# FFN1 eight slots behind the attention, its end blocks side by side, x split one pair a slot; w_in converted thinly, then densely; ten pairs by rows with float32 value products

## The chip, the cores and the metric

The kernel runs on one core of a Trainium2 chip. The time is that of the device, in microseconds (us), from launch to end; the kernel before took 1503.16 us, the median of three runs (1502.47 to 1505.43). The core has five engines that run their own instruction streams and wait for each other by semaphores: TensorE (PE; its weight loads are listed as PEld), VectorE (DVE), ScalarE (ACT), GpSimd (POOL) and SyncE (SP), which here only issues the transfers (DMAs). TensorE writes to PSUM, eight banks here called bank0 to bank7; the other tiles lie in SBUF.

## The reference

Attention with RMS-normalised queries and keys, and behind it a feed-forward network with a squared ReLU:

```python
q_n, k_n = (rmsnorm(q, g_q), rmsnorm(k, g_k))     # q, k, v: 8 x 12 x 448 x 64, float32
scores = scale * np.matmul(q_n, k_n.transpose(0, 1, 3, 2))
scores = scores - np.max(scores, axis=-1, keepdims=True)
attn = np.exp(scores)
attn = attn / (np.sum(attn, axis=-1, keepdims=True) + 1e-09)
out = np.matmul(attn, v)
x = out, laid out as 3584 tokens x 768
h = x @ w_in                                      # 768 x 2048
r = np.maximum(h, 0.0)
g = s * (r * r) + b
return g @ w_out                                  # 2048 x 768
```

w_in and w_out come as 64-bit floating-point numbers; the kernel rebuilds float32 values from their two words, which is called a conversion below.

## The kernel before

**Precision.** TensorE's fast format (float32r) keeps fewer bits than float32. A product is therefore made of three: high part by high part, high by low, low by high. So every large operand has to be split into a high part (a cast, mostly on ScalarE) and a low part (value minus high part, on VectorE or GpSimd). The float32 product is the other way: one instruction, without a split, that TensorE runs as two passes.

**Slots.** The 96 heads are 48 pairs (NPAIR), six to a batch (NP) of eight (B). The whole attention is one list of slots, written out by hand with a fixed order of instructions on all five engines (manual_schedule, L612). A pair has eight slots (W), four chunks of keys for each of its two heads; slot s handles chunk s. In a slot PE makes the transposed scores of the chunk in two products (score_t, L398), the scores in the other direction of the chunk ten slots ahead (score, L362; AHEAD), whose maximum VectorE takes (maximum, L374), and the value products of the chunk two slots before (weigh, L449). ScalarE takes the exponential (exponent). All other work of a pair is put at fixed distances from its first slot by at(...) in the loop at L565: loading, normalising and splitting its queries and keys before, and taking the sums, their reciprocals (gather, invert, divide, by way of DRAM) and the result u after. A job started in one slot may go on in the next ones, one step a slot (the list begun, L630). Jobs in the list late (L550) come last in the slot on VectorE and GpSimd.

**Two ways for queries and keys.** Pairs of the first batch (p < NP) come by rows: load_rows, norm_rows (square on ScalarE, sums on VectorE, power and scaling on GpSimd), turn (eight transpositions on PE a head) and split_turned. The others come already transposed and twice (load_kq), with their inverse roots computed from a second load (load, norm), kept in DRAM and spread over the partitions (keep, spread), multiplied in scale and split in split_kq.

**Two ways for the value products.** For the pairs p < NV, 12 here, exponentials and values stay float32 (load_v, weigh: one product a chunk). For the others exponentials are split (split_e on ScalarE, split_e_lo on VectorE), values too (split_v), and a chunk has three products, the last chunk of a head, which packs high and low parts into the same rows, two.

**FFN1.** ffn_in (L174) makes one block of 128 of the 2048 hidden columns for one batch: 6 x 3 matmuls into one bank. The 16 blocks of a batch are a stream from which each slot takes six matmuls (FILL = 2, 2, 2): 48 slots use up 288. The stream of batch b - 1 begins START = 13 slots behind that batch's last slot (L654). What it reads, x split into two parts, is made by split_x (L510), two pairs at a time, in the three slots before and at that begin. rectify applies the ReLU on ScalarE and frees the bank, keep_r stores the result in DRAM.

**w_in.** Its 24 pieces of 128 x 512 are loaded (load_piece, L530) and converted in slots s to s + 4 for each s in PACE (L32): four operations on VectorE, two on ScalarE, one on GpSimd (load_double, L116). Two buffers each hold the raw words (w64) and the value being built (wa). Six entries of PACE lie before slot 6, then one every five slots up to slot 91.

**Behind the slots.** FFN1 of the last batch runs alone on PE, while w_out is converted, 32 pieces, two a step (L731; later_by, four steps, is how far the last part of a conversion stands behind the others, since it writes over w_in). ffn_out (L697) then makes FFN2 from tiles g = s r^2 + b, three tiles together at first, then one by one; its instructions are ordered by the framework, not by hand.

Of the kernel before, what the change touches and what calls it, by code (L numbers as in the profile page):

```python
# [11 lines left out]
I32 = mybir.dt.int32  # L12
# [8 lines left out]

LEAST = (1 + 1 / 8) * 2.0 ** (0x70 - 127)

START = 13

AHEAD = 10

# [1 line left out]

FILL = (2, 2, 2)  # L30

PACE = (-18, -14, -10, -6, -2, 2, *range(6, 92, 5))  # L32

GAP = 2

# [2 lines left out]
def attention_then_relu2_ffn(  # L38
# [38 lines left out]
    NP = NPAIR // B  # L77
    H = 2 * NP
    TILES = 2 * SEQ // P
    NV = 2 * NP  # L80
    NQ = 4
    QC = SEQ // NQ
    REST = SEQ % P
# [87 lines left out]
    xp = ctx.enter_context(tc.tile_pool(name="xpool", bufs=1))  # L171
    later = []

    def ffn_in(xs, b, fc):  # L174

        i, f0 = divmod(fc * P, FS)
        ph, bank = psum(f"ph{b}_{fc}")
        n = 0
        for cc in range(NCC):
            for w, part in ((whi[i], 0), (wlo[i], 0), (whi[i], 1)):  # L180
                T.matmul(  # L181
                    ph[:, :SEQ],
                    w[:, cc, f0 : f0 + P],
                    xs[b, cc][:, part, :],
                    start=n == 0,
                    stop=n == 3 * NCC - 1,
                )
                n += 1
                if n == 3 * NCC:
                    later.append((ph, bank, b, fc))  # L190
                yield

    def rectify():

# [15 lines left out]
    with tc.tile_pool(name="apool", bufs=1) as ap:  # L210
# [296 lines left out]

        xs = {}

        def split_x(b, k):  # L510
            for g in (2 * k, 2 * k + 1):
                u = us.pop(b * NP + g)
                x = xs[b, g] = xp.tile([P, 2, SEQ], F32R, tag=f"x{g}", name=f"x{b}_{g}")
                S.copy(x[:, 0, :], u)
                V.tensor_tensor(x[:, 1, :], u, x[:, 0, :].bitcast(F32), ALU.subtract)  # L515

        def pieces():
            for i, (hi, lo, src) in enumerate(parts_of_w_in()):
# [15 lines left out]
                next(g)  # L534
                loaded.append(g)

        def convert(n):


            g = loaded[0] if n == 0 else turning[0]  # L540
            if n == 0:
                turning.append(loaded.pop(0))
            for _ in range((2, 1, 1, 2, 1)[n]):
                next(g, None)
            if n == 4:
                turning.pop(0)

        turning = []

        late = (convert, invert)  # L550

# [12 lines left out]

        for p in range(NPAIR):  # L565
            s0 = W * p
            if p >= NP:
                at(s0 - 32, load, p)
                at(s0 - 28, norm, p)
                at(s0 - 24, keep, p)  # L570
            for j in range(2):
                s1 = s0 + 4 * j
                if p >= NP:
                    at(s1 - 19, load_kq, p, j)
                    at(s1 - 19, spread, p, j)
                    at(s1 - 15, scale, p, j)
                    at(s1 - 13, split_kq, p, j)
                else:
                    at(max(s1 - 28, FIRST), load_rows, p, j)
                    at(s1 - 20, norm_rows, p, j)  # L580
                    at(s1 - 13, turn, p, j)
                    at(s1 - 12, split_turned, p, j)
                at(s1 - 10, double_kb, p, j)
                at(s1 - 6, shift, p, j)
                at(s1 + 6, take, p, j)
                at(s1 + 7, gather, p, j)
            at(s0 - (9 if p >= NV else 5), load_v, p)
            if p >= NV:
                at(s0 - 3, split_v, p)
            at(s0 + 13, invert, p)  # L590
            at(s0 + 14, divide, p, 1)
            at(s0 + 16, divide, p, 2)
            at(s0 + 18, divide, p, 3)
        for b in range(B):
            for k_ in range(3):
                at(W * NP * (b + 1) + START - 2 + k_, split_x, b, k_)
        for _ in range(2):
            at(FIRST + 1, load_piece)
        for s_ in PACE:
            for n in range(5):  # L600
                at(s_ + n, convert, n)
            at(s_ + 3, load_piece)

        def within(i):
# [6 lines left out]
        sb_b = cpool.tile([P, 1], F32, name="sb_b")  # L611
        with tc.manual_schedule(engines=ORDERED):  # L612
            begun = []
            for s_ in range(FIRST, NSLOT + START + 1):
                if s_ == FIRST:
                    nc.sync.dma_start(gg, g_qk)
                    V.scalar_tensor_tensor(gqk, gg[:, 0:1], D**-0.5, gg[:, 1:2], ALU.mult, ALU.mult)
                if s_ == 0:
                    for t, x in ((sb_s, s), (sb_b, b_)):
                        nc.sync.dma_start(t, x.rearrange("(o d) -> o d", o=1).broadcast_to([P, 1]))  # L620
                if s_ in (FIRST, FIRST + 4):
                    warm_up(30)
                if within(s_):
                    score_t(s_)
                filler(FILL[0])
                if within(s_ - 1):
                    split_e(s_ - 1)
                if within(s_):
                    exponent(s_)
                begun = [g for g in begun if next(g, 0) is None]  # L630
                keep_r()
                for f, a in jobs[s_]:
                    if f in late:
                        continue
                    g = f(*a)
                    if g is not None and next(g, 0) is None:
                        begun.append(g)
                ahead = s_ + AHEAD
                scored = within(ahead)
                if scored:  # L640
                    score(ahead)
                filler(FILL[1])
                rectify()
                if within(s_ - 1):
                    split_e_lo(s_ - 1)
                if scored:
# [12 lines left out]
            rectify()
            keep_r()  # L660


    with tc.tile_pool(name="opool", bufs=2) as op:

        def pieces():
            for i, part in enumerate(parts_of_w_out()):
                w = op.tile([P, WO, 2], I32, tag="w64", bufs=4, name=f"w64o{i}")
                m = op.tile([P, WO], F32, tag="wm", bufs=2, name=f"wmo{i}")

                def words(i=i):  # L670
                    return op.tile([P, WO], I32, tag="wa", bufs=10, name=f"wao{i}")

                yield load_double((w, words, m), *part, apart=True, rest=V)

# [47 lines left out]
        pieces = pieces()  # L722


        later_by = NFC // NS
        with tc.manual_schedule(engines=ORDERED - {ENGINE.SP}):
            waiting = []
            todo = list(islice(pieces, 2))
            for g in todo:
                next(g)  # L730
            for m in range(NFC + later_by):  # L731
                if m < NFC:
                    for _ in ffn_in(xs, *units[m]):
                        pass
                now, todo = todo, list(islice(pieces, 2))
                for g in todo:
                    next(g)
# [69 lines left out]
```

## Time and profile before

| what | value |
|---|---|
| median of three runs | 1503.16 us |
| span of the profiled execution, first to last instruction | 1504.4 us |
| TensorE busy | 1452.9 us, 97% |
| VectorE busy | 874.7 us, 58% |
| ScalarE busy | 786.3 us, 52% |
| GpSimd busy | 689.9 us, 46% |
| mean granted clock of TensorE | 0.988 |
| transfers | 230.83 MB, 153 GB/s in the mean |

A profile is one execution recorded by the hardware. Its page gives busy time by engine, the chain of work that ended last (followed back from the last instruction, at each step to what released it), and the groups of instructions: a line of the code, engine, operation, what it writes and reads, the shapes, the count, then the busy time, the mean in ns, and the idle time of that engine just before, with what ended it. The trace behind it answers by windows of time, by waits, and as a timeline. Times in it are us from the first instruction. Two things to keep in mind: matmuls are pipelined, so one whose mean is 367 ns may follow the one before it by 203; and a mean over the whole span mixes stages with different limits, here the slots without FFN1, the slots with it, and FFN2.

### The profile page before, as it was taken

The numbers are of one execution on the slowest core, as the hardware profiler recorded it, in microseconds if no ns is written. First come the engines' busy times: TensorE is split into PE (matmuls) and PEld (weight loads), VectorE is DVE, ScalarE is ACT, GpSimd is POOL, SyncE is SP. The second block draws the span as 40 slices with busy tenths as digits, with TensorE's granted clock in tenths as the row PEclk, the third lists the DMA queues.
The fourth block names the chain that finished last, engine by engine and source line by source line (L and its number), as shares of the span: only waits on it lengthen the run. The fifth ranks groups of instructions, "written<-read, shape, count | busy, mean of one in ns | idle before, by whom it ended". The sixth has DMA issues, their size and how long they took to land.

```text
span 1504.4 us, 21397 instructions
## 1 busy us (share of the span) xinstructions
PE 1452.9 (97%) x7344; PEld 1330.3 (88%) x7344; DVE 874.7 (58%) x1319; ACT 786.3 (52%) x1436; POOL 689.9 (46%) x569
## 2 busy tenths in 40 slices
PE   6887899999999999999999999999999999999998
PEld 6555688899899889889989989999999999999998
DVE  6998876766766676676676665289532222222210
ACT  3675555766766766766676676446432222222210
POOL 6589888777677677777777764100000000000000
PEclk8898999999999999999999999999999999999999
DMA  4468776566566666666656652188333233223200
GB/s 140 110 180 230 214 234 190 167 198 193 175 196 190 193 175 194 191 190 191 183 168 195 191 173 91 67 295 255 113 105 78 80 101 90 78 87 100 84 22 32
DMA packets 221916, 230.83 MB, mean 153 GB/s; under 512 B 78896, under 2 KB 199728, under 8 KB 221808
## 3 DMA queue, kind: packets, MB, share of 16 engines
q1 hardware_dynamic: 221808, 229.47, 51.8%
q8 instruction: 58, 0.95, 0.3%
q14 instruction: 50, 0.41, 0.1%
HBM read 177.21 MB, written 40.84 MB: 145 GB/s over the span
## 4 chain that ended last, share of the span: by engine, by line
PE 88%; DVE 5%; DMA 3%; issue 1%; ACT 1%; POOL 1%; SPq 0%; DVEq 0%; POOLq 0%; ACTq 0%
PE po L706 31%; PE ph L181 30%; PE av L465 13%; PE st L406 4%; PE st L409 4%; PE sh L368 4%; DVE x L515 2%; PE warmth L272 1%; DVE nmx L379 1%; DMA zt<-uz 1%; DMA z_d<-zt 1%; DMA rb<-i_d 0%; DVE al L446 0%; DVE wai L134 0%; DVE wai L129 0%
## 5 line engine op out<-in xcount | busy, mean ns | idle before, releaser
L181 PE MATMUL ph<-x,wih 128*128 128x448 f32 x1536 | 490.9, 367 | 2.6 <-DVE x L515 2.2
L181 PEld LDWEIGHTS ph<-x,wih 128*128 128x128 f32 x1536 | 289.0, 188 | 33.6 <-issue 6.4
L379 DVE TENSOR_REDUCE nmx<-sh 112x1 fp32r<-112x448 f32 x384 | 236.6, 619 | 136.0 <-PE sh L368 130.9
L181 PE MATMUL ph<-x,wil 128*128 128x448 f32 x768 | 294.1, 383 | 0.0
L425 ACT ACTIVATE st<-st 128x448 f32<-128x448 f32 (+1 forms) x288 | 151.1, 525 | 220.8 <-PE st L409 204.2
L706 PE MATMUL po<-woh,gh 128*128 128x384 f32 x896 | 228.0, 334 | 0.0
L706 PE MATMUL po<-wol,gh 128*128 128x384 f32 x896 | 228.0, 334 | 0.0
L706 PE MATMUL po<-woh,gl 128*128 128x384 f32 x896 | 227.7, 334 | 0.0
L368 PE MATMUL sh<-ka,qa 128*112 128x448 f32 x384 | 147.1, 385 | 30.5 <-ACT wih L137 12.5
L465 PE MATMUL av<-ah,vs 128*128 128x448 f32 x576 | 164.3, 366 | 0.1
L406 PE MATMUL st<-qa,ka 128*128 128x448 f32 (+1 forms) x384 | 163.5, 426 | 0.5 <-ACT e L421 0.5
L706 PEld LDWEIGHTS po<-woh,gh 128*128 128x128 f32 x896 | 161.7, 188 | 0.4 <-ACT r L198 0.3
L706 PEld LDWEIGHTS po<-wol,gh 128*128 128x128 f32 x896 | 161.8, 188 | 0.0
L706 PEld LDWEIGHTS po<-woh,gl 128*128 128x128 f32 x896 | 161.8, 188 | 0.0
L181 PEld LDWEIGHTS ph<-x,wil 128*128 128x128 f32 x768 | 144.4, 188 | 17.8 <-issue 6.9
L433 ACT CAST ah<-st 128x448 fp32r<-128x448 f32 (+1 forms) x288 | 154.1, 535 | 1.8
L446 DVE TENSOR_TENSOR al<-st,ah 128x448 fp32r<-128x448 f32 x216 | 132.1, 611 | 35.6 <-ACT ah L433 21.7
L368 PEld LDWEIGHTS sh<-ka,qa 128*112 128x112 f32 x384 | 107.6, 281 | 42.5 <-ACT wih L137 15.8
L688 ACT ACTIVATE r<-r 128x2048 f32<-128x2048 f32 x28 | 53.7, 1919 | 172.9 <-DMA r<-r_d 172.8
L409 PE MATMUL st<-qb,kb 128*128 128x448 f32 (+1 forms) x384 | 141.4, 368 | 0.0
L352 POOL TENSOR_TENSOR ka<-kq,ka 64x448 fp32r<-64x448 f32 x84 | 99.0, 1179 | 91.8 <-ACT ka L349 88.4
L689 DVE TENSOR_SCALAR r<-r,sb_s,sb_b 128x2048 f32<-128x2048 f32 x28 | 37.6, 1345 | 173.0 <-ACT r L688 173.0
(75 smaller groups left out, 2181.2 us busy)
## 6 DMA issues: line engine op xcount, KB each, us to landing
kq<-in_dram SPq DMA_DIRECT2D x84, 448.0 KB, 4.4
rb<-i_d SPq DMA_DIRECT2D x84, 448.0 KB, 5.7
r_d<-r SPq DMA_DIRECT2D x128, 224.0 KB, 2.5
r<-r_d SPq DMA_DIRECT2D x24, 1024.0 KB, 5.9
raw<-in_dram SPq DMA_DIRECT2D x42, 448.0 KB, 5.0
w64i<-in_dram SPq DMA_DIRECT2D x24, 512.0 KB, 4.9
w64o<-in_dram SPq DMA_DIRECT2D x32, 384.0 KB, 5.1
kb<-ka SPq DMA_DIRECT2D x96, 112.0 KB, 3.8
```

The lines of the kernel that those rows point to most:

```text
L181: T.matmul(ph[:, :SEQ], w[:, cc, f0 : f0 + P], xs[b, cc][:, part, :], start=n == 0, stop=n == 3 * NCC - 1,)
L352: G.tensor_tensor(ka[n][D:, a], t[D:, 0], ka[n][D:, a].bitcast(F32), ALU.subtract)
L368: T.matmul(sh[:QC, :SEQ], qa[p % 2][:, a].rearrange("k (p c) -> k c p", c=NQ)[:, c], ka[p % 2][:, a], start=True, stop=True,)
L379: V.tensor_reduce(out=nmxs[p][:, c : c + 1], in_=sh[:QC, :SEQ], op=ALU.max, axis=AX.X, negate=True)
L406: T.matmul(st[:rows, :SEQ], ka[n][:, keys], qa[n][:, q], start=True, stop=False)
L409: T.matmul(st[:rows, :SEQ], kb[n][:, keys], qb[n][:, q], start=False, stop=True,)
L425: S.activation(st[:rows, :SEQ], st[:rows, :SEQ], AF.Exp)
L433: S.copy(ah[:rows], sts[i][0][:rows, :SEQ])
L446: V.tensor_tensor(al, st[:rows, :SEQ], ah[:rows].bitcast(F32), ALU.subtract)
L465: T.matmul(av[:, :SEQ], x, a, start=kc == 0 and m == 0, stop=kc == 3 and m == len(todo) - 1,)
L688: S.activation(r, r, AF.Square)
L706: T.matmul(po[e][0][:, :HALF], x[:, fc, :], w[:, f, e * HALF : (e + 1) * HALF], start=fc == 0 and m == 0, stop=fc == NFC - 1 and m == 2,)
```

## The change

- START goes from 13 to 8. split_x handles one pair a slot, in six slots from START - 1 on, and the list of slots still ends at the same slot, 397.
- ffn_in takes a list of blocks and interleaves them by pair of x: the first two blocks of a batch, and the last two, run side by side, each in a bank of its own. Six matmuls, one slot, then use one pair of x. The last batch begins inside the slots, and the loop behind takes the rest from the same stream.
- PACE: one piece at slot -16, then one every six slots from -5 to 55, then twelve from slot 57 on, alternately two and three slots apart (57, 59, 62, 64, ... 84). The conversions are told apart by their number, as more than one can be under way.
- Pairs 0 to 9 (TURNED) come by rows, not 0 to 5; pairs 0 to 9 (PLAIN) have float32 value products, not 0 to 11.
- One warm-up of 30 products is left of two.
- Behind the slots: later_by is 2, not 4, and wa there has 6 buffers, not 10.

```diff
-START = 13
+START = 8
-PACE = (-18, -14, -10, -6, -2, 2, *range(6, 92, 5))
+PACE = (-16, *range(-5, 57, 6), *(57 + 5 * i // 2 for i in range(12)))
+TURNED = 10
+PLAIN = 10
...
-    NV = 2 * NP
+    NV = PLAIN
...
-    def ffn_in(xs, b, fc):
+    def ffn_in(xs, b, fcs):
+        phs = [psum(f"ph{b}_{fc}") for fc in fcs]
         for cc in range(NCC):
-            for w, part in ((whi[i], 0), (wlo[i], 0), (whi[i], 1)):
+            for (ph, bank), fc in zip(phs, fcs):
+                i, f0 = divmod(fc * P, FS)
+                for m, (w, part) in enumerate(((whi[i], 0), (wlo[i], 0), (whi[i], 1))):
...
+    def ffn_in_batch(xs, b):
+        blocks = ((0, 1), *((fc,) for fc in range(2, NFC - 2)), (NFC - 2, NFC - 1))
+        return chain.from_iterable(ffn_in(xs, b, fcs) for fcs in blocks)
...
-        def split_x(b, k):
-            for g in (2 * k, 2 * k + 1):
-                u = us.pop(b * NP + g)
...
+        def split_x(b, g):
+            u = us.pop(b * NP + g)
+            x = xs[b, g] = xp.tile([P, 2, SEQ], F32R, tag=f"x{g}", name=f"x{b}_{g}")
+            S.copy(x[:, 0, :], u)
+            V.tensor_tensor(x[:, 1, :], u, x[:, 0, :].bitcast(F32), ALU.subtract)
...
-        def convert(n):
-            g = loaded[0] if n == 0 else turning[0]
...
+        def convert(i, n):
             for _ in range((2, 1, 1, 2, 1)[n]):
-                next(g, None)
+                next(loaded[i], None)
...
-            if p >= NP:
+            if p >= TURNED:
...
-            for k_ in range(3):
-                at(W * NP * (b + 1) + START - 2 + k_, split_x, b, k_)
-        for _ in range(2):
-            at(FIRST + 1, load_piece)
-        for s_ in PACE:
+            for g in range(NCC):
+                at(W * NP * (b + 1) + START - 1 + g, split_x, b, g)
+        for s_ in (-18, -10):
+            at(s_, load_piece)
+        for i, s_ in enumerate(PACE):
             for n in range(5):
-                at(s_ + n, convert, n)
+                at(s_ + n, convert, i, n)
             at(s_ + 3, load_piece)
...
-                if s_ in (FIRST, FIRST + 4):
+                if s_ == FIRST:
                     warm_up(30)
...
-                    units = [(b - 1, fc) for fc in range(NFC)]
-                    fill = chain.from_iterable(ffn_in(xs, *u) for u in units) if b < B else iter(())
+                    fill = ffn_in_batch(xs, b - 1)
...
-                    return op.tile([P, WO], I32, tag="wa", bufs=10, name=f"wao{i}")
+                    return op.tile([P, WO], I32, tag="wa", bufs=6, name=f"wao{i}")
...
-        later_by = NFC // NS
+        later_by = 2
...
-                if m < NFC:
-                    for _ in ffn_in(xs, *units[m]):
-                        pass
+                filler(NCC * 3)
```

On the host, the rows of pairs 0 to 9 are laid out in place of those of the first batch, and the zeros that the float32 products need stand in the values of ten pairs.

More of the change, by code (lines that the diff above doesn't have):

```diff
@@ L172, in attention_then_relu2_ffn @@
     later = []
-    def ffn_in(xs, b, fc):
-        i, f0 = divmod(fc * P, FS)
-        ph, bank = psum(f"ph{b}_{fc}")
-        n = 0
+    def ffn_in(xs, b, fcs):
+        phs = [psum(f"ph{b}_{fc}") for fc in fcs]
         for cc in range(NCC):
-            for w, part in ((whi[i], 0), (wlo[i], 0), (whi[i], 1)):
[L181 to L191, printed above, removed]
+            for (ph, bank), fc in zip(phs, fcs):
+                i, f0 = divmod(fc * P, FS)
+                for m, (w, part) in enumerate(((whi[i], 0), (wlo[i], 0), (whi[i], 1))):
+                    T.matmul(
+                        ph[:, :SEQ],
+                        w[:, cc, f0 : f0 + P],
+                        xs[b, cc][:, part, :],
+                        start=cc == 0 and m == 0,
+                        stop=cc == NCC - 1 and m == 2,
+                    )
+                    if cc == NCC - 1 and m == 2:
+                        later.append((ph, bank, b, fc))
+                    yield
+    def ffn_in_batch(xs, b):
+        blocks = ((0, 1), *((fc,) for fc in range(2, NFC - 2)), (NFC - 2, NFC - 1))
+        return chain.from_iterable(ffn_in(xs, b, fcs) for fcs in blocks)
     def rectify():
@@ L508, in attention_then_relu2_ffn @@
         xs = {}
-        def split_x(b, k):
-            for g in (2 * k, 2 * k + 1):
-                u = us.pop(b * NP + g)
-                x = xs[b, g] = xp.tile([P, 2, SEQ], F32R, tag=f"x{g}", name=f"x{b}_{g}")
-                S.copy(x[:, 0, :], u)
-                V.tensor_tensor(x[:, 1, :], u, x[:, 0, :].bitcast(F32), ALU.subtract)
+        def split_x(b, g):
[3 more added lines that the diff above has]
+            V.tensor_tensor(x[:, 1, :], u, x[:, 0, :].bitcast(F32), ALU.subtract)
         def pieces():
@@ L535, in load_piece @@
                 loaded.append(g)
-        def convert(n):
-            g = loaded[0] if n == 0 else turning[0]
-            if n == 0:
-                turning.append(loaded.pop(0))
+        def convert(i, n):
             for _ in range((2, 1, 1, 2, 1)[n]):
-                next(g, None)
-            if n == 4:
-                turning.pop(0)
-        turning = []
+                next(loaded[i], None)
         late = (convert, invert)
@@ L572, in attention_then_relu2_ffn @@
                 s1 = s0 + 4 * j
-                if p >= NP:
+                if p >= TURNED:
                     at(s1 - 19, load_kq, p, j)
@@ L613, in attention_then_relu2_ffn @@
             begun = []
-            for s_ in range(FIRST, NSLOT + START + 1):
+            for s_ in range(FIRST, NSLOT + START + NCC):
                 if s_ == FIRST:
@@ L786 @@
     vs = v.reshape(n, 2, s, d)[:, :, keys].transpose(0, 3, 2, 1, 4)
-    vs[: 2 * n // b, : p // 2, 3] = 0
+    vs[:PLAIN, : p // 2, 3] = 0
     g = _np.stack([_np.tile(_np.asarray(inputs[x]), 2) for x in ("g_q", "g_k")], 1)
-    rows0 = _np.stack([a[0].reshape(n // b, 2, 4, s // 4, d) for a in (k, q)], 2)
+    rows0 = _np.stack([a.reshape(n, 2, 4, s // 4, d)[:TURNED] for a in (k, q)], 2)
     rows0 = rows0.transpose(0, 4, 1, 2, 3, 5)
```

## The prediction, made before the changed kernel was run

> **What bounds the kernel now.** I read the page first: TensorE is busy for 97% of the span. That alone would leave no room, so I then took the sums by window over the stretches in which the work differs. Columns: window, its length, then busy time and instruction count of PE, PEld, DVE, ACT and POOL, granted clock, DMA share, GB/s.
>
> ```profile
> core 0: us, PE busy (x) PEld busy (x) DVE busy (x) ACT busy (x) POOL busy (x), PEclk, DMA share, GB/s
> 18.30:37.00 18.70, 8.71 (x45) 6.92 (x44) 16.69 (x27) 10.40 (x18) 12.14 (x12) 0.67 0.51 147
> 37.00:60.50 23.50, 19.01 (x69) 13.32 (x67) 21.27 (x31) 15.57 (x30) 13.35 (x13) 0.82 0.42 113
> 60.50:104.80 44.30, 40.07 (x170) 27.55 (x169) 41.20 (x69) 32.60 (x63) 35.72 (x34) 1.00 0.55 150
> 104.80:151.10 46.30, 35.18 (x108) 22.75 (x106) 40.59 (x55) 24.57 (x48) 42.16 (x39) 0.89 0.82 224
> 151.10:172.90 21.80, 18.03 (x61) 11.78 (x60) 19.47 (x25) 13.61 (x28) 19.12 (x15) 0.92 0.75 222
> 172.90:260.00 87.10, 87.10 (x375) 70.87 (x374) 62.82 (x86) 46.40 (x90) 73.06 (x61) 1.00 0.73 212
> 280.00:300.00 20.00, 18.15 (x87) 15.72 (x86) 14.69 (x25) 15.23 (x32) 13.57 (x10) 1.00 0.52 163
> 300.00:320.00 20.00, 20.00 (x100) 18.39 (x99) 13.89 (x22) 13.75 (x28) 14.99 (x13) 1.00 0.65 193
> ```
>
> Next the chain of work that ended last (start, length, what) and the timeline, for the real cost of a matmul and the places of the slots:
>
> ```profile
> 84.24 0.77 PE tk L246 x8
> 228.36 0.75 PE av L465 x2
> 345.85 0.61 PE av L465 x3
> 961.58 72.15 PE ph L181 x356
> 1033.73 9.04 PE po L706 x52
> 1042.79 457.20 PE po L706 x2636
> ```
> ```profile
> 2.29 16.24 PE L272 MATMUL warmth<-ident 128*128 128x128 f32 x120 [2.29 <-POOL ident masks.py:199]
> 8.39 1.43 POOL L239 TENSOR_TENSOR rows<-rows,ri 112x512 f32<-112x512 f32 x1
> 37.03 0.57 PE L406 MATMUL st<-qa,ka 128*128 128x448 f32 x1
> 151.09 0.71 PE L406 MATMUL st<-qa,ka 128*128 128x448 f32 x1
> ```
>
> Slot 0 begins at 37.03, slot 56 at 151.09. From 961.58 on PE runs 356 FFN1 matmuls in 72.15 us, 0.203 each, then FFN2 without a gap. A transposition of eight is 0.77, a value product of one chunk 0.75 in float32 (two passes) and 0.61 as three split products (0.41 in every fourth chunk, which has two; 0.56 on average). A slot without FFN1 holds one maximum product, two score products and a value product: 3 x 0.203 + 0.75 = 1.36 us of PE. Slots 0 to 55 took 114.1 us, 2.04 each: PE is not the bound there, whatever its busy time says (stalled matmuls count as busy). VectorE is: 103.1 of the 114.1 us (21.27 + 41.20 + 40.59). From 172.9 on PE is full, except where x is split: 87 instructions in 280:300 against 100 in 300:320, so 13 x 0.2 = 2.6 us lost, at each of six batch changes.
>
> **The change, in five stretches.** Prices of VectorE, first in the stretch with rows alone, then beside FFN1 (mean ns behind the busy time):
>
> ```profile
> L129 DVE SCALAR_TENSOR_TENSOR wai<-w64i,wai 128x512 int32<-128x512 int32 x5 | 5.4, 1086 | 0.2
> L126 DVE TENSOR_SCALAR wai<-w64i 128x512 int32<-128x512 int32 x5 | 3.5, 709 | 0.0
> L131 DVE SCALAR_TENSOR_TENSOR wai<-w64i,wai 128x512 int32<-128x512 int32 x5 | 3.4, 679 | 0.0
> L234 DVE TENSOR_REDUCE ssq<-sq 112x8 f32<-112x512 f32 x5 | 3.4, 672 | 0.1
> L134 DVE SCALAR_TENSOR_TENSOR wai<-wih,wai 128x512 f32<-128x512 f32 x4 | 3.0, 748 | 0.0
> L310 DVE TENSOR_REDUCE ssq<-raw 128x14 f32<-128x896 f32 x2 | 2.2, 1086 | 0.2
> L331 DVE SCALAR_TENSOR_TENSOR kq<-kq,gqk,rb 128x448 f32<-128x448 f32 x1 | 1.0, 1029 | 0.0
> ```
> ```profile
> L379 DVE TENSOR_REDUCE nmx<-sh 112x1 fp32r<-112x448 f32 x36 | 22.3, 619 | 22.5 <-PE sh L368 22.3
> L331 DVE SCALAR_TENSOR_TENSOR kq<-kq,gqk,rb 128x448 f32<-128x448 f32 x9 | 12.7, 1411 | 1.0 <-DMA rb<-i_d 1.0
> L129 DVE SCALAR_TENSOR_TENSOR wai<-w64i,wai 128x512 int32<-128x512 int32 x7 | 9.0, 1292 | 0.2
> L134 DVE SCALAR_TENSOR_TENSOR wai<-wih,wai 128x512 f32<-128x512 f32 x7 | 6.7, 953 | 0.0
> L131 DVE SCALAR_TENSOR_TENSOR wai<-w64i,wai 128x512 int32<-128x512 int32 x7 | 5.7, 818 | 0.0
> L126 DVE TENSOR_SCALAR wai<-w64i 128x512 int32<-128x512 int32 x6 | 3.4, 564 | 0.0
> ```
>
> A piece of w_in thus costs VectorE 3.22 us there and 3.63 here.
>
> *Start to slot 0, now 37.0.* The second warm-up goes: half of 16.24 us, 8.1. The first transposition needs the scaled rows, done at 9.82, so it can start near 10.4. Behind it VectorE was busy 16.69 of 18.7 us with three w_in pieces in it; one remains (PACE has -16 and -5 in place of five entries before slot 0), 6.4 us less, but POOL's scaling of the next rows and the way to ScalarE and back then show. I take 3 us more: **26**, between 22 (all 14.5) and 31 (6 only).
>
> In the Trainium skill, "TensorE: Matmul & The Clock Gate", Part 1, the array is throttled by default and a busy window releases it, which speaks against dropping a warm-up. The rows show 0.67 in 18.3:37, although the warm-up ran until 18.5; so it did not hold the clock then either. By the page I would add some 3 us here (an estimate from 0.93 us for a transposition at full rate): 29 in place of 26.
>
> *Slots 0 to 55, now 114.1.* Pairs 6 to 9 come by rows, and a piece is turned every 6 slots in place of 4 to 5. The nearest row is 60.5:104.8: 24 slots (11 to 34) by rows, 41.20 us of VectorE, 3.1 idle. One piece of five less (-3.2), the scaling and two row sums of the other path out (-1.0 - 2.2), one row sum in (+0.7): 35.5 + 3.1 = 38.6, 1.61 per slot. PE's own floor is near: 1.36 + 0.77/4 = 1.55. With two engines so close I take 1.74, halfway between 1.61 and the 1.85 that the row shows now: **97.5**; the ends are 90 (1.61) and 107 (the first 11 slots as slow as now, 23.5/11, the others at 44.3/24). The DMA share of 0.82 in 104.8:151.1, with the loads of 448 KB, falls to something like the 0.55 of the rows; ScalarE gets 1.6 us per pair more, which its 32.60 of 44.30 holds.
>
> *Slot 56 to the last value product, now 961.6 - 151.1 = 810.5.* FFN1 begins at slot 56, not 61. (a) 151.1:172.9 covers slots 56 to 63 and needs of PE only 5 x 1.36 + 3 x 2.57 = 14.5 of 21.8: -7.3. (b) One pair of x a slot, and two blocks side by side that consume one pair a slot: the six losses of 2.6 go, -15.6. (c) 30 more FFN1 matmuls lie in this stretch: +6.1. (d) Pair 9's two transpositions fall here: +1.5. (e) Pairs 10 and 11 split: 16 x (0.75 - 0.56) = -3.0. Sum 792.2. What is late next: at a batch change VectorE carries 13.89/20 of 2.39, 1.66 a slot, and x adds
>
> ```profile
> L515 DVE TENSOR_TENSOR x<-u,x 128x448 fp32r<-128x448 f32 x48 | 39.6, 867 | 27.7 <-ACT x L514 27.7
> ```
>
> 0.87: 2.5 for a slot of 2.39 over six slots: **+1** (0 to 6). (f) The dense pieces, slots 57 to 88. VectorE: 12 pieces x 3.63 = 43.6; 32 maxima, 19.8; six scalings x 1.41 = 8.5; four row sums, 4.3; eight splits of exponentials of pair 10 at 0.61, 4.9; four of x, 3.5; pair 9's rows and the reciprocals, 4.8: 89.4. At the 93 to 95% that it reached above, 94 us. PE needs 25 x 2.57 + 7 x 2.39 + 1.5 = 82.5. So **+12** (3, if the lag of a slot hides it, to 24, if pieces cost 4.6). A piece now meets its buffer wa (two) five slots after it was last taken, and POOL must have finished with it: VectorE would wait, behind it the maxima, and PE for their banks. POOL has 73.06 of 87.1 us; five pieces more in these 82 us, at 1.28, make it some 92%. A piece's load is issued two slots ahead, 5.1 us, and lands in 4.9:
>
> ```profile
> L140 POOL TENSOR_TENSOR wil<-wai,wih 128x512 fp32r<-128x512 f32 x7 | 9.0, 1281 | 0.2
> w64i<-in_dram SPq DMA_DIRECT2D x24, 512.0 KB, 4.9
> 13.65 0.69 DVE L134 SCALAR_TENSOR_TENSOR wai<-wih,wai 128x512 f32<-128x512 f32 x1
> 31.65 2.21 DVE L134 SCALAR_TENSOR_TENSOR wai<-wih,wai 128x512 f32<-128x512 f32 x1
> ```
>
> The last two rows are one operation of VectorE alone and beside POOL (the second ran while POOL scaled rows).
>
> The Trainium skill, "SBUF — State Buffer", section "Who interferes with whom", has VectorE and GpSimd share a port pair as an exclusive lock: "Whoever issues first gets the shared pair for the whole instruction". The two rows agree. By the rule the dense stage, with POOL near full, would pay the 2.21 more often than the mean does; that is the last rival.
>
> *Tail, now 1504.4 - 961.6 = 542.8.* 30 matmuls less before FFN2 would give 6.1. But w_out is turned by VectorE, beginning behind the last x:
>
> ```profile
> 972.96 4.63 DVE L515 TENSOR_TENSOR x<-u,x 128x448 fp32r<-128x448 f32 x6 [7.10 <-ACT x L514]
> 1041.58 2.28 DVE L694 TENSOR_TENSOR gl<-r,gh 128x2048 fp32r<-128x2048 f32 x1
> 1062.20 3.83 DVE L140 TENSOR_TENSOR wol<-wao,woh 128x384 fp32r<-128x384 f32 x8
> ```
>
> The third g tile is ready at 1043.9, 82.3 us after the last value product. FFN2 asks for it 48 matmuls of 0.174 after its begin: now at 80.5, then at 74. The last of w_out is done at 1066.0, 104.4 behind, and FFN2's last quarter asks for it at 109.7 now, then at 104. That chain starts from pair 47's reciprocals, which nothing shortens; FFN1 ending 6 us sooner only waits for it. **-0.5** (-6 to +4): 542.3.
>
> **Sum:** 26 + 97.5 + 792.2 + 1 + 12 + 542.3 = 1471.0 by this execution's span of 1504.4. The median of the runs, 1503.16, is 1.2 below it: **1470**, 2.2% faster.
>
> **The rivals.**
> - *Dense stage hidden and tail gained.* VectorE lags by under a slot and FFN2's order lets it start early: -9 and -5.5: 1455. For it: 22.3 us in which maxima waited for PE in the 87 us beside FFN1. Against: 89.4 us of work in 82.5. 12%.
> - *The early slots keep their pace.* Another bound takes over (half clock, the way rows-PE-ACT-DVE-PE, the transfers of the reciprocals): 107 as above, and slot 0 at 29: +9.5 + 3: 1483. For it: PE 40.07 of 44.30 in the rows. 17%.
> - *Only shifted.* Each piece not turned early is paid at full price in the dense stage and the wait for x stays: 97.5 + 10, +15 at the changes, dense 20 instead of 12: 1503, no change. Against: six losses of 2.6 stand at lines that the change rewrites. 2%.
> - *Slower: lock-step in the dense stage.* All three two-input operations of a piece run into POOL at 2.21: a piece costs 0.56 + 6.63 = 7.2 in place of 3.63, +43: 1513. It decides from 6.4 us a piece on. For it: POOL near 92%, two buffers. Against: in 104.8:151.1 POOL had 42.16 of 46.30 and no such price. 4%.
> - The forecast itself, 1457 to 1483: 65%.
>
> **How the numbers follow.** Ends of the range: 1452 (head 22, slots 1.65, half of the dense cost) and 1492 (1.9 a slot, dense 20); it takes in the first two rivals. About 0.2% is what a measurement of this kernel can tell from no change: faster 0.94, same 0.02, slower 0.04.
>
> **What would show it.** Slot 0 near 26 and slot 56 near 124 in the timeline; about 100 instructions per 20 us at the batch changes; between slots 57 and 88 VectorE over 90% busy, a few us of gaps on PE; the last value product near 929, and a gap of PE at the start of FFN2. Wrong if w_in pieces cost VectorE over 5 us each in the dense stage, if PE idles behind x still, or if slots 0 to 55 need over 107 us.

## The result and the profile after

The changed kernel takes **1480.43 us** in the median of four runs (1479.64 to 1485.01), beside 1504.3 for the kernel before (four runs, 1502.47 to 1506.6): a ratio of **0.9846, 95% interval 0.9828 to 0.9863**. It is faster by 1.5%, and lies 10.4 us above the forecast, within its range.

The page of after, its first line and its busy times:

```profile
span 1477.8 us, 21404 instructions
...
PE 1443.6 (98%) x7360; PEld 1328.2 (90%) x7360; DVE 863.5 (58%) x1347; ACT 799.8 (54%) x1466; POOL 687.8 (47%) x559
```

TensorE's share says as little as before: it has 9 us less busy time in a span 26.6 us shorter. The sums by window of after tell more (columns as in the prediction). The rows are the start up to slot 0, slots 0 to 55, 56 to 63 and 64 to 87, then 20 us in which x is split and 20 us behind that:

```profile
core 0: us, PE busy (x) PEld busy (x) DVE busy (x) ACT busy (x) POOL busy (x), PEclk, DMA share, GB/s
10.00:27.75 17.75, 9.52 (x58) 7.69 (x56) 15.54 (x27) 8.51 (x15) 12.93 (x14) 0.81 0.37 99
27.75:122.79 95.04, 91.64 (x390) 64.22 (x388) 84.48 (x148) 74.92 (x147) 79.13 (x76) 0.98 0.52 142
122.79:153.31 30.52, 25.26 (x106) 19.18 (x105) 22.96 (x39) 16.69 (x32) 23.00 (x17) 0.94 0.46 121
153.31:221.50 68.19, 63.21 (x270) 51.70 (x269) 61.55 (x86) 42.89 (x84) 55.84 (x43) 0.97 0.76 228
259.79:279.79 20.00, 19.29 (x93) 17.03 (x92) 17.86 (x29) 15.79 (x35) 15.86 (x12) 1.00 0.62 180
281.00:301.00 20.00, 20.00 (x100) 18.40 (x99) 13.47 (x22) 14.05 (x29) 14.17 (x13) 1.00 0.69 199
```

Slot 0 starts at 27.75 (37.03 before), slot 56 at 122.79 (151.09). So 28.3 us are won ahead of FFN1, more than the 26.6 of the whole: behind slot 56 the kernel is no better than before. A batch change still costs PE instructions, 93 against 100.

The same cuts for every run that follows, by the starts of the first score product of a slot in the timeline. "Changes" is what the groups of eight slots from slot 96 on take beyond the 19.15 us of an undisturbed group. "Tail" begins at the last value product. The time is the median; the ratio is that to the kernel before on the same chip.

| run | time us | ratio, 95% | slot 0 | 0 to 55 | 56 to 63 | 64 to 87 | changes | tail |
|---|---|---|---|---|---|---|---|---|
| before | 1504.3 | | 37.0 | 114.1 | 21.8 | 61.6 | 16.2 | 543.1 |
| after | 1480.4 | 0.9846 (0.9828 to 0.9863) | 27.8 | 95.0 | 30.5 | 68.2 | 7.8 | 539.2 |
| e1 | 1507.7 | 1.0024 (1.0014 to 1.0033) | 36.4 | 112.2 | 25.9 | 64.0 | 14.0 | 545.0 |
| e2 | 1486.9 | 0.9889 (0.9871 to 0.9907) | 27.0 | 103.7 | 27.8 | 68.8 | 7.9 | 539.5 |
| e3 | 1481.9 | 0.9852 (0.9835 to 0.9868) | 28.0 | 95.0 | 30.4 | 64.0 | 9.3 | 538.8 |
| e4 | 1487.8 | 0.9891 (0.9876 to 0.9905) | 31.2 | 111.0 | 26.4 | 60.9 | 8.0 | 538.7 |
| e5 | 1478.9 | 0.9835 (0.9821 to 0.9849) | 28.4 | 96.4 | 26.7 | 69.2 | 7.9 | 539.4 |
| e6 | 1468.8 | 0.9767 (0.9754 to 0.9781) | 27.7 | 94.9 | 27.9 | 66.6 | 0.0 | 540.6 |
| e7 | 1477.4 | 0.9824 (0.981 to 0.9838) | 27.3 | 95.1 | 30.6 | 66.0 | 7.9 | 538.4 |
| e8 | 1467.1 | 0.9753 (0.974 to 0.9766) | 27.6 | 97.9 | 26.5 | 66.0 | 0.0 | 538.1 |
| e9 | 1491.6 | 0.9917 (0.9894 to 0.994) | 28.3 | 95.0 | 28.6 | 69.5 | 13.5 | 542.9 |
| e10 | 1510.0 | 1.0031 (1.0019 to 1.0042) | 36.7 | 114.0 | 19.9 | 61.7 | 19.8 | 543.3 |
| e11 | 1487.4 | 0.9881 (0.9863 to 0.9899) | 32.0 | 95.0 | 30.7 | 69.8 | 7.9 | 539.5 |
| e12 | 1469.8 | 0.9765 (0.9751 to 0.978) | 27.9 | 95.9 | 27.5 | 66.7 | 0.0 | 539.2 |

Two waits carry what was not won. The timeline of after shows the first at the begin of the dense pieces and the second at a batch change (start, length, engine, line, operation; in brackets the idle time of the engine before it and what ended it):

```profile
134.35 2.26 POOL L246 TENSOR_TENSOR rows<-rows,ri 112x512 f32<-112x512 f32 x1
...
136.58 2.83 POOL L513 TENSOR_TENSOR u<-uz,zb 64x448 f32<-64x448 f32 x2
...
140.06 1.27 POOL L144 TENSOR_TENSOR wil<-wai,wih 128x512 fp32r<-128x512 f32 x1
...
141.36 0.43 DVE L130 TENSOR_SCALAR wai<-w64i 128x512 int32<-128x512 int32 x1 [4.20 <-POOL wil L144]
...
141.59 0.47 PE L185 MATMUL ph<-x,wih 128*128 128x448 f32 x1 [1.98 <-ACT x L520]
...
259.91 0.63 DVE L521 TENSOR_TENSOR x<-u,x 128x448 fp32r<-128x448 f32 x1 [2.86 <-ACT x L520]
...
260.45 0.62 DVE L453 TENSOR_TENSOR al<-st,ah 128x448 fp32r<-128x448 f32 x1
```

At 137.2 VectorE wants the buffer wa for the next piece. GpSimd works through its own list (rows until 136.6, then u, then zeros) before it takes the piece in that buffer, so VectorE stands for 4.2 us. At a batch change VectorE reaches the subtraction of x before ScalarE has made the cast that it subtracts. VectorE takes its work in order, so it stands for 2.9 us, and the exponentials (al, at 260.45) and the maxima behind it stand with it. The waits of VectorE in after, first 122 to 225, then 255 to 282 (line, released by: us in total, times, longest):

```profile
DVE wai L130 <- POOL wil L144: 5.4, 2, 4.2
...
DVE wai L130 <- DMA w64i<-in_dram: 2.5, 2, 2.1
```
```profile
DVE x L521 <- ACT x L520: 4.5, 4, 2.9
```

### The profile page after: what moved, and what is told of

Same layout as the page of the kernel before. It is cut to its first block, busy times and chain, and to the rows that moved or that the text cites. A ratio compares the mean times of both kernels' runs of the same rounds, so it can differ in the third digit from the quotient of the medians.

```text
span 1477.8 us, 21404 instructions
## 1 busy us (share of the span) xinstructions
PE 1443.6 (98%) x7360; PEld 1328.2 (90%) x7360; DVE 863.5 (58%) x1347; ACT 799.8 (54%) x1466; POOL 687.8 (47%) x559
## 4 chain that ended last, share of the span: by engine, by line
PE 82%; DVE 8%; DMA 3%; issue 2%; POOL 2%; ACT 2%; SPq 0%; POOLq 0%; ACTq 0%; DVEq 0%
PE po L703 31%; PE ph L185 24%; PE av L472 13%; PE sh L375 5%; PE st L413 4%; PE st L416 4%; DMA w64o<-in_dram 1%; DMA w64i<-in_dram 1%; DVE nmx L386 1%; DVE kq L338 1%; PE tk L253 1%; DVE x L521 1%; DVE wao L133 1%; DVE ssq L317 1%; DVE al L453 1%
## 5 line engine op out<-in xcount | busy, mean ns | idle before, releaser
L386 DVE TENSOR_REDUCE nmx<-sh 112x1 fp32r<-112x448 f32 x384 | 237.2, 620 | 114.0 <-PE sh L375 111.3
L185 PE MATMUL ph<-x,wil 128*128 128x448 f32 x768 | 291.1, 379 | 0.0
L432 ACT ACTIVATE st<-st 128x448 f32<-128x448 f32 (+1 forms) x304 | 159.4, 524 | 222.0 <-PE st L416 219.3
L472 PE MATMUL av<-ah,vs 128*128 128x448 f32 x608 | 173.9, 367 | 3.6 <-DVE al L453 3.6
L440 ACT CAST ah<-st 128x448 fp32r<-128x448 f32 (+1 forms) x304 | 162.6, 535 | 1.6
L453 DVE TENSOR_TENSOR al<-st,ah 128x448 fp32r<-128x448 f32 x228 | 139.6, 612 | 36.9 <-ACT ah L440 24.1
L413 PE MATMUL st<-qa,ka 128*128 128x448 f32 (+1 forms) x384 | 158.0, 411 | 1.0 <-ACT e L428 0.9
L513 POOL TENSOR_TENSOR u<-uz,zb 64x448 f32<-64x448 f32 x96 | 123.0, 1281 | 40.0 <-DMA zb<-z_d 36.4
```

Source lines behind the costliest of these rows:

```text
L185: T.matmul(ph[:, :SEQ], w[:, cc, f0 : f0 + P], xs[b, cc][:, part, :], start=cc == 0 and m == 0, stop=cc == NCC - 1 and m == 2,)
L386: V.tensor_reduce(out=nmxs[p][:, c : c + 1], in_=sh[:QC, :SEQ], op=ALU.max, axis=AX.X, negate=True)
L413: T.matmul(st[:rows, :SEQ], ka[n][:, keys], qa[n][:, q], start=True, stop=False)
L432: S.activation(st[:rows, :SEQ], st[:rows, :SEQ], AF.Exp)
L440: S.copy(ah[:rows], sts[i][0][:rows, :SEQ])
L453: V.tensor_tensor(al, st[:rows, :SEQ], ah[:rows].bitcast(F32), ALU.subtract)
```

## The experiments

My theory after the result: the time behind slot 56 goes to VectorE's in-order waits at the batch changes and to the dense pieces. The rival: to the change's other parts (the stream of FFN1, the value products, a clock that lacks the second warm-up). e1 to e4 and e11 take the change apart, e5 to e8 take the two waits away, e9 and e10 ask what carries the batch changes, e12 tries for more.

**e1: the kernel before, with the new stream of FFN1 alone** (blocks side by side, x one pair a slot; later_by 2 and the six buffers wa behind the slots come with it). By its diff against after:

```diff
-START = 8
+START = 13
-PACE = (-16, *range(-5, 57, 6), *(57 + 5 * i // 2 for i in range(12)))
-TURNED = 10
-PLAIN = 10
+PACE = (-18, -14, -10, -6, -2, 2, *range(6, 92, 5))
+TURNED = 6
+PLAIN = 12
...
-        for s_ in (-18, -10):
-            at(s_, load_piece)
+        for _ in range(2):
+            at(FIRST + 1, load_piece)
...
-                if s_ == FIRST:
+                if s_ in (FIRST, FIRST + 4):
```

> The kernel before with the new FFN1 stream alone: x split one pair a slot, the end blocks side by side, later_by 2; the start of FFN1, the w_in pieces, the rows, the value products and both warm-ups as before. My theory: the loss at each of the six batch changes falls from 2.6 us to the 1.3 us that the changed kernel shows (8 us in all), and some 3 us of the wait at FFN1's begin go: 1493 us. Rival, that the x split alone carries the whole gain: 1486 or less. Rival, that it only shifts a wait: 1503.

Measured: 1507.7, slower than before by 0.24% (0.14 to 0.33%). The theory and the first rival fell; the second, that a wait is only shifted, comes nearest. The waits of PE in e1, 148 to 177, where FFN1 begins:

```profile
PE ph L185 <- ACT x L520: 3.2, 1, 3.2
PE ph L185 <- DVE x L521: 3.0, 1, 3.0
```

The one-pair stream takes only 2.2 us off the changes (16.2 to 14.0), and pays 4.1 and 2.4 in slots 56 to 87 and 1.9 in the tail. With START at 13 it saves nothing. How much of the tail's part comes from the smaller later_by was not tried alone.

**e2: pairs 6 to 9 not by rows.**

```diff
-TURNED = 10
+TURNED = 6
```

> The changed kernel with pairs 6 to 9 loaded and scaled as before, not by rows. My theory: rows carry the faster slots 36 to 55 (2.0 to 2.2 us each before, 1.75 now), so slots 0 to 55 take 8 to 12 us more, and the 1.5 us of transpositions in the FFN1 slots are saved: 1488 to 1491 us. Rival, that the thin conversions carry these slots and rows cost TensorE 6 us of transpositions: 1475 us.

```profile
27.02:130.67 103.65, 89.39 (x341) 60.07 (x340) 87.08 (x137) 70.77 (x138) 89.03 (x81) 0.98 0.65 184
```

This is slots 0 to 55 of e2 in the sums by window. They take 103.7 in place of 95.0: the rows bring 8.7 there, 6.5 in the whole. It is less than the 9.5 that separate the forecast 97.5 from the rival's 107, but the rows do carry these slots. They do it less by VectorE's load, which is only 2.6 us higher in e2 (87.08 to 84.48), than by waits of the other path. Two waits of e2, 27 to 130.7, that do not occur in the same slots of after:

```profile
PE sh L375 <- POOL ka L359: 7.7, 4, 3.0
```
```profile
DVE kq L338 <- DMA rb<-i_d: 5.4, 3, 2.4
```

**e3: twelve pairs with float32 value products.**

```diff
-PLAIN = 10
+PLAIN = 12
```

> The changed kernel with float32 value products for 12 pairs as before. My theory: TensorE gets 3.0 us more work, VectorE loses the 0.61 us per chunk in slots 81 to 97, which cover two waits of 1.6 and 2.2 us in slots 82 and 86, so nearly no change: 1478 to 1482 us. Rival, that TensorE alone counts there: 1483.4 us.

Measured: 1481.9, no change to after. Splitting pairs 10 and 11 brings nothing in the end. Without it slots 64 to 87 are 4.2 shorter, but not for want of exponentials to split: 3.9 of it lie in slots 64 to 81 (46.2 in place of 50.1), ahead of the first of these. It is the loss in slot 75, 6.2 us long in after, that e3 does not have; VectorE's wait for late loads of w_in, 2.5 us there (122 to 225), is 0.2 in e3. Against that, slots 88 to 95 take 20.5 in place of 19.1, and the changes 1.5 more.

**e4: the pieces evenly spread**, with two loads at the very first.

```diff
-PACE = (-16, *range(-5, 57, 6), *(57 + 5 * i // 2 for i in range(12)))
+PACE = (-18, -14, -10, -6, -2, 2, *(6 + 14 * i // 3 for i in range(18)))
...
-        for s_ in (-18, -10):
-            at(s_, load_piece)
+        for _ in range(2):
+            at(FIRST + 1, load_piece)
```

> The changed kernel with the w_in pieces at the old density, six before slot 6 and then one every 4.7 slots up to slot 85. My theory: the waits between slots 56 and 88 (about 16 us now) shrink to 3 or 4, and the slots before 56 carry 4.5 pieces more at 3.2 us of VectorE, 14 us: 1481 us, with slot 0 about 5 us later, and slots 0 to 55 at 1.85 each. Rival, that VectorE has room in the early slots: 1468 us. Rival, that the thin start brings more than its weight: 1490 us.

Measured: 1487.8, between the two, nearer to the rival. Slots 0 to 55 of e4 in the sums by window, then two groups of VectorE there (count, busy us and mean ns), then the same two in after:

```profile
31.15:142.15 111.00, 94.40 (x389) 65.63 (x388) 104.69 (x162) 77.99 (x151) 83.34 (x80) 0.97 0.47 131
```
```profile
L138 DVE SCALAR_TENSOR_TENSOR wai<-wih,wai 128x512 f32<-128x512 f32 x12 | 16.5, 1374 | 0.0
L133 DVE SCALAR_TENSOR_TENSOR wai<-w64i,wai 128x512 int32<-128x512 int32 x13 | 15.3, 1175 | 0.4
```
```profile
L133 DVE SCALAR_TENSOR_TENSOR wai<-w64i,wai 128x512 int32<-128x512 int32 x9 | 7.0, 772 | 0.3
L138 DVE SCALAR_TENSOR_TENSOR wai<-wih,wai 128x512 f32<-128x512 f32 x9 | 6.4, 706 | 0.0
```

Four pieces more cost VectorE 20.2 us, as each of the thirteen costs 3.81 (with 0.706 and 0.559 for its other two operations) in place of 2.79. Most of the rise is in L138 (1.374 in place of 0.706), and what raises it stands in the timeline of e4, at 40 to 44:

```profile
40.52 1.53 POOL L246 TENSOR_TENSOR rows<-rows,ri 112x512 f32<-112x512 f32 x1
...
41.60 2.23 DVE L138 SCALAR_TENSOR_TENSOR wai<-wih,wai 128x512 f32<-128x512 f32 x1
42.01 1.27 POOL L144 TENSOR_TENSOR wil<-wai,wih 128x512 fp32r<-128x512 f32 x1
```

VectorE's operation starts while GpSimd scales rows, some 1.1 us after that began, and lasts through GpSimd's next operation too, 2.23 us in place of some 0.68. In e4 five of the twelve operations of L138 meet these two GpSimd operations in this way, and all five take 2.23. In after none of the nine does: eight take 0.64 to 0.68, four of them though they begin together with a row scaling. So pieces every six slots are worth more than their number. The Trainium skill, "SBUF — State Buffer", section "Who interferes with whom", says that a VectorE instruction with two inputs in SBUF contends with a GpSimd instruction that reads SBUF; the rows above agree. Other rows of e4 do not, and there the measurement decides: GpSimd's power, which reads SBUF too, lasts through the whole of the same operation, and it takes 0.67 us:

```profile
86.87 1.95 POOL L245 TENSOR_TENSOR ri<-ri,mhalf 112x8 f32<-112x8 f32 x1
...
87.78 0.67 DVE L138 SCALAR_TENSOR_TENSOR wai<-wih,wai 128x512 f32<-128x512 f32 x1
```

**e5, e6, e7, e8: the waits behind slot 56.** e5 puts the thin pieces two slots earlier, so that wa is free when the dense ones begin; e6 gives the cast of x a step of its own; e7 issues a piece's load one slot earlier; e8 has all three.

```diff
-PACE = (-16, *range(-5, 57, 6), *(57 + 5 * i // 2 for i in range(12)))
+PACE = (-16, *range(-7, 55, 6), *(57 + 5 * i // 2 for i in range(12)))
```
```diff
             S.copy(x[:, 0, :], u)
+            yield
             V.tensor_tensor(x[:, 1, :], u, x[:, 0, :].bitcast(F32), ALU.subtract)
...
-                at(W * NP * (b + 1) + START - 1 + g, split_x, b, g)
+                at(W * NP * (b + 1) + START - 2 + g, split_x, b, g)
```
```diff
-            at(s_ + 3, load_piece)
+            at(s_ + 2, load_piece)
```

> The changed kernel with the thin pieces two slots earlier (-7 to 53), so that no piece meets its buffer wa less than five slots after its last user began; the changed kernel has four slots between 55 and 59. My theory: VectorE's wait of 4.2 us for GpSimd's last step of the piece of slot 55, which holds x and the maxima behind it, goes, and slot 61 shrinks from 8.25 us to 3.5 or less: 1475 to 1477 us. Rival, that VectorE's own load is the bound in slots 57 to 63: unchanged, 1480 us.

> The changed kernel with ScalarE's cast of x one slot earlier, and VectorE's subtraction first in the slot after it, so at the same slot as now. My theory: at a batch change the loss of 1.3 us is VectorE standing 2.9 us before a subtraction whose cast ScalarE has not made yet, with the other work queued behind it; that wait goes, six times 1.3 us at most: 1473 to 1476 us. Rival, that VectorE simply has more work than a slot there (2.5 us for 2.39): unchanged, 1480 us.

> The changed kernel with each w_in load issued one slot earlier, which the two buffers w64 just allow. My theory: VectorE's wait of 2.1 us for a piece in slot 74 and the 3.6 us that TensorE loses in slot 75 go in part: 1477 to 1479 us. Rival, that the dense pieces' VectorE time is what counts: unchanged, 1480 us.

> The three edits together. My theory, that they take away different waits: 1466 to 1471 us, with the stretch from slot 56 to 64 near 24 us and the batch changes without loss. Rival, that VectorE's load takes their place: 1476 or more.

e5: 1478.9, short of its expectation, and no clear change to after (the intervals overlap). The wait of 4.2 is gone and slots 56 to 63 are 3.8 shorter, but slots 0 to 55 give back 1.4, and the waits of VectorE in e5, 122 to 225, show that the loads are late instead (2.5 before):

```profile
DVE wai L130 <- DMA w64i<-in_dram: 4.9, 3, 2.3
```

e6: **1468.8**, beyond its expectation. The loss at the changes goes from 7.8 to 0.0, and slots 56 to 87, in which the x of the first batch is split, are 4.2 us shorter as well. A batch change of e6 in the sums by window, and VectorE's wait for the cast, 245 to 270:

```profile
247.50:267.50 20.00, 20.00 (x100) 18.39 (x99) 17.97 (x29) 16.14 (x34) 14.69 (x12) 1.00 0.59 175
```
```profile
DVE x L522 <- ACT x L520: 1.1, 2, 0.7
```

VectorE is as loaded as in after (17.97 and 17.86 of 20), and PE has its 100 instructions. So it was the wait and not the load.

e7: 1477.4, 3 us less and as expected, but the intervals overlap. e8: 1467.1, as expected, and the lowest time of all; its slots 56 to 63 take 26.5 us, not the 24 expected. These slots, 64 to 87 and 88 to 95 of e8 in the sums by window:

```profile
125.47:151.93 26.46, 23.81 (x107) 18.27 (x105) 24.58 (x38) 16.29 (x32) 21.44 (x17) 1.00 0.57 162
151.93:217.92 65.99, 62.76 (x270) 51.99 (x269) 63.96 (x86) 43.03 (x84) 59.61 (x44) 0.97 0.75 227
217.92:237.06 19.14, 19.14 (x95) 17.61 (x94) 13.27 (x22) 13.31 (x29) 16.59 (x14) 1.00 0.69 196
```

VectorE is busy for 24.58 of 26.46 and 63.96 of 65.99 us. With the waits gone its work is what is left in the dense stage, and a piece there costs more, 3.87 in place of 3.33 (by its four groups, as below for after). VectorE's lag does not hold PE everywhere: slots 64 to 81 of e8 take 46.2 us, 2.57 each, which is PE's own time. Most of the loss behind slot 63 comes at slots 82 and 83, 9.6 us together, the first in which PE needs the low part of pair 10's exponentials from VectorE. PE's wait for it in e8, 125.4 to 238:

```profile
PE av L472 <- DVE al L453: 3.2, 2, 2.9
```

The three together bring 1.7 us more than e6 alone. e8 with float32 value products for pairs 10 and 11 was not tried.

**e9: x at the old place.**

```diff
-START = 8
+START = 13
```

> The changed kernel with FFN1 13 slots behind as before, all else as changed. My theory: the place of x among a pair's slots sets the loss at a batch change, 2.3 us as in the FFN1 stream alone against 1.3 us at START = 8, so +6 us there; and slots 56 to 60 go without FFN1, some 3 us of TensorE's idle time more; the tail has its 6 us of matmuls back but waits less: 1488 to 1491 us. Rival, that START only moves work about: 1481.

**e10: the kernel before, its casts of x a slot ahead of the subtractions**, still two pairs a slot.

```diff
+            todo_x = []
             for g in (2 * k, 2 * k + 1):
...
                 S.copy(x[:, 0, :], u)
-                V.tensor_tensor(x[:, 1, :], u, x[:, 0, :].bitcast(F32), ALU.subtract)
+                todo_x.append((x, u))
+            yield
+            for x, u in todo_x:
+                V.tensor_tensor(x[:, 1, :], u, x[:, 0, :].bitcast(F32), ALU.subtract)
...
-                at(W * NP * (b + 1) + START - 2 + k_, split_x, b, k_)
+                at(W * NP * (b + 1) + START - 3 + k_, split_x, b, k_)
```

> The kernel before with one edit: ScalarE's two casts of x one slot earlier, VectorE's two subtractions first in the slot after; still two pairs a slot, three slots, FFN1 13 slots behind. My theory: the 2.6 us at each of six batch changes are VectorE standing 3.2 us before a cast that ScalarE has not made; without that wait 10 to 16 us go: 1489 to 1494 us. Rival, that two subtractions in a slot are simply too much VectorE work (1.7 us on 1.66 in 2.39): 1501 or more.

e9: 1491.6, at the upper end of its expectation; the changes cost 13.5, 2.25 each, in place of 7.8. So it is START at 8 that takes most off the loss, not the one pair a slot. In after x falls into slots 7 to 12 of 48; with START at 13 it falls into 12 to 17. In an undisturbed period of after VectorE is busiest in the sixth slot of a pair, where scaling and reciprocals meet right behind the row sums (2.80 us in slot 149); slot 13 is such a slot, and lies in 12 to 17 alone. That this makes the difference was not tried by itself.

e10: 1510.0, slower than before by 0.31% (0.19 to 0.42%); the rival that I gave it holds. VectorE's wait for the cast, 282 to 304, falls from 3.2 to 0.7, yet the changes cost 19.8:

```profile
DVE x L519 <- ACT x L515: 0.7, 1, 0.7
```
```profile
287.00:291.70 4.70, 2.73 (x13) 2.15 (x13) 4.67 (x9) 2.82 (x7) 3.82 (x3) 1.00 0.61 229
```

The second row is one slot of e10 in the sums by window: 4.70 us long, VectorE busy for 4.67. The slot holds two subtractions of x beside row sums, scaling and reciprocals. There it is the load, and with one pair a slot at START 8 it is the wait. Both must go, and only e6 and the two runs built on it have neither. Which of the two, the second pair or the place, makes the load of e10 was not tried apart.

**e11: two warm-ups.**

```diff
-                if s_ == FIRST:
+                if s_ in (FIRST, FIRST + 4):
```

> The changed kernel with the second warm-up of 30 products. My theory: slot 0 comes 5 to 6 us later (the rest of the 9.3 us gained there was the thin start: 31.15 with the denser pieces, 27.75 now), and all behind it with it: 1486 us. Rival, that the second warm-up keeps the clock up in the first slots: slots 0 to 55 then shorter by the same, 1480.

Measured: 1487.4, near the 1486 expected, with slot 0 4.3 us later and not 5 to 6; where the rest of the 7.0 us lies was not followed. Slots 0 to 55 of e11 in the sums by window:

```profile
32.01:127.02 95.01, 90.75 (x389) 63.69 (x388) 84.49 (x148) 74.90 (x147) 79.12 (x76) 0.99 0.52 141
```

They take 95.01 us, beside 95.04 with one warm-up, at a granted clock of 0.99 and 0.98. The second warm-up buys nothing there. The Trainium skill, "TensorE: Matmul & The Clock Gate", Part 1, has the throttle released by a busy window; by these rows one warm-up and the work behind it are enough for slots 0 to 55.

**e12: e8 with the dense pieces every three slots from 56 to 89.**

```diff
-PACE = (-16, *range(-7, 55, 6), *(57 + 5 * i // 2 for i in range(12)))
+PACE = (-16, *range(-7, 55, 6), *range(56, 92, 3))
```

> The three edits of the run before and the dense pieces three slots apart, from slot 56 to 89, not two and three. My theory: the 5.5 us that slots 64 to 88 still take over TensorE's own time shrink to 2, and 56 to 64 gains a little: 1462 to 1465 us. Rival, that a looser spacing only moves the load on to the slots with split exponentials: 1467.

Measured: 1469.8, not the gain that I expected. Slots 88 to 95 of e12 in the sums by window:

```profile
217.98:238.68 20.70, 19.45 (x96) 17.52 (x95) 17.09 (x26) 14.20 (x30) 15.61 (x12) 1.00 0.59 168
```

They take 20.70 us, 19.14 in e8. It is not VectorE that is full there (17.09 us). FFN1's last blocks of a batch read the last piece of w_in, which now begins at slot 89, and PE waits in slot 94 for GpSimd to finish it. The waits of PE in e12, 123.8 to 239:

```profile
PE av L472 <- DVE al L453: 3.2, 1, 3.2
...
PE ph L185 <- POOL wil L144: 1.3, 1, 1.3
```

The first row is the wait for the exponentials' low part, as in e8, now in slot 86. The time lies beyond the rival's 1467 too, and the rival's reason holds for this wait alone. e8 keeps the lowest time, though the two intervals overlap.

## Why the prediction was right, and where it was off

The direction and the place were right: the gain lies ahead of slot 56, in the stretch where VectorE was the bound. Point by point, against the sum of 1471.0 by the span:

- *Start to slot 0:* 26 forecast, **27.75** measured. The second warm-up is worth 4.3 to 5.2 us (e11 to after; e1 at 36.36 to e4 at 31.15), not 8.1. To halve the 16.24 us was wrong: the first warm-up alone takes 9.34, so the first transposition begins 6.9 us earlier than before (18.37), at 11.47 and not near 10.4. Two rows of after:

```profile
2.30 9.34 PE L279 MATMUL warmth<-ident 128*128 128x128 f32 x60 [2.30 <-POOL ident masks.py:199]
11.47 0.93 PE L253 MATMUL tk<-ident,rows 112*64 112x112 f32 x8
```

  What takes up the rest until slot 0 was not tried apart. The pieces and their loads bring 3.4 (e4 to after), near the net 3.4 (6.4 less 3) of the forecast. The granted clock from 10 us to slot 0 did not fall with the warm-up, 0.81 in place of 0.77, and the 29 that stands beside the sum was 1.25 too high.
- *Slots 0 to 55:* 97.5 forecast, **95.0** measured; the rival with 107 is out. The row of 24 slots by rows held (e2), though what rows save is more in waits than in VectorE's load. What I had not seen is that thinner pieces also get cheaper, 2.79 us each (e4).
- *Slot 56 on:* 805 forecast, **815.8** measured. This is where it failed, **in the step (b), "the six losses of 2.6 go, -15.6", and in the "+1 (0 to 6)" that it left as late next.** The six changes still cost 7.8. I priced VectorE's load at a change, 2.5 us a slot, and not that VectorE stands in order for ScalarE's half of the split; the row that I quoted for x had "27.7 <-ACT x L514" in it. e6 takes the wait and leaves the load, and the loss is 0.0. The +1 was also added up wrongly: 0.14 us over six slots at each of six changes make 5; that this is nearer to the 7.8 is luck, as the load was not the cause. A second reading in that step was wrong too: one pair a slot saves little by itself (e1, e9); its place does.
- *Dense pieces (f):* 12 forecast, **16** measured: 30.5 where PE needs 22.1 (14.5 + 6.1 + 1.5 of the prediction), 68.2 where it needs some 60.6 (61.6 before, less the first of the split value products). The mechanism was right, and the named wait for wa occurred: the dense piece of slot 59 meets the buffer of slot 55 after four slots, and not five. The piece was dearer in the forecast than in fact; four groups of after, 122 to 225:

```profile
L133 DVE SCALAR_TENSOR_TENSOR wai<-w64i,wai 128x512 int32<-128x512 int32 x13 | 13.8, 1058 | 0.4
L138 DVE SCALAR_TENSOR_TENSOR wai<-wih,wai 128x512 f32<-128x512 f32 x13 | 11.1, 856 | 0.0
L135 DVE SCALAR_TENSOR_TENSOR wai<-w64i,wai 128x512 int32<-128x512 int32 x13 | 10.3, 792 | 0.0
L130 DVE TENSOR_SCALAR wai<-w64i 128x512 int32<-128x512 int32 x13 | 8.1, 625 | 7.9 <-POOL wil L144 5.4 <-DMA w64i<-in_dram 2.5
```

  They add up to 3.33 us, 3.63 in the forecast. The lock-step rival decided from 6.4 on, so it is out. What exceeds the 12 are waits that no term held: the 7.9 us in the last row, and that for the cast of x. With all of them gone (e8) slots 56 to 87 take 92.4 us in place of 98.7.
- *Tail:* -0.5 forecast, **-3.9** measured (543.1 to 539.2). The forecast let FFN2 lose nearly all that FFN1 gives, to the third tile of g. That wait occurred, but it is short. FFN2 begins at 1005.72, right behind FFN1, and stands once, for 1.0 us, before that tile; in the timeline of after:

```profile
1005.72 0.51 PE L703 MATMUL po<-woh,gh 128*128 128x384 f32 x2
...
1014.52 1.33 DVE L686 TENSOR_SCALAR r<-r,sb_s,sb_b 128x2048 f32<-128x2048 f32 x1
...
1016.39 1.91 ACT L690 CAST gh<-r 128x2048 fp32r<-128x2048 f32 x1
...
1018.35 0.62 PE L703 MATMUL po<-woh,gh 128*128 128x384 f32 x2 [1.00 <-ACT gh L690]
```

  Before it PE makes 66 matmuls of FFN2, not the 48 of the prediction, so it asks later; and it waits for ScalarE's cast, not for VectorE's part of g. FFN1 behind the last value product is 5.2 us shorter (72.15 to 66.92), FFN2 1.3 longer. How much of it is the smaller later_by was not tried alone.
- *Span and median:* a run lies 1.8 us above its own span here (1479.64 for 1477.8). I had set 1.2 below, from the median of before against the span of one profiled run: 3 us of the miss, and the plainest of its errors.

The terms close: +1.8 at the start, -2.5, +6.8 at the changes, +4 in the dense stage, -3.1 in the tail and -0.2 in the rest make 6.8, the distance of the spans (1477.8 less 1471.0); 3.0 from the offset and 0.8 from this execution to the median make the 10.6 from the unrounded 1469.8.

The ends of the range do not follow from the terms named for them: these give 1455 and 1487, not 1452 and 1492. The measured time lies inside both.

The rivals: *only shifted* is out by the spans. *Dense stage hidden and tail gained* holds only in part of its tail. The interplay was none of them: undone one by one, the rows cost 6.5, the pace 7.3, the warm-up 7.0, and START 11.2, together 32 of a gain of 24, and the new stream alone costs 3.4. Those are differences of medians without an interval, some taken on different chips.

## What to carry to other kernels

When work is split between two engines, price the in-order wait of the second for the first, and not only the load of each; where a row shows such a wait now, the change must move one of the halves to a step of its own, or the wait comes along. A cost per slot hides where in the period the slot lies: shift the work by a few slots before thinning it. Parts of a change are not additive: the stream of FFN1 loses alone and carries the best version.

## What the runs showed of the hardware

- The price of one piece on VectorE went from 2.79 to 3.81 us with the spacing of the pieces alone (after and e4). In the rows of e4 VectorE's operation lasted through two GpSimd operations that followed each other without a gap (40.52 to 43.28), not through one; five of twelve did, and took 2.23 us each.
- A GpSimd operation beside it does not always cost VectorE time: beside GpSimd's power of 1.95 us (86.87 in e4) the same operation took 0.67. The row at 13.65 that the prediction calls VectorE alone has such a power beside it too (GpSimd, 12.24 to 14.33), and took 0.69.
- A second warm-up of TensorE put the first transposition off by 6.0 us (17.48 in e11, 11.47 in after), and changed slots 0 to 55 from 95.04 us into 95.01.
